# Attention and spectral mixing on one core: one PSUM layout for two parts, and three early score pairs

## The chip, the cores and the metric

The kernel runs on one core of one Trainium2 chip. The metric is the device time of one execution in microseconds; the time before is the median of three runs. A profile of one more execution gives start and duration of every instruction. In its rows PE is the matrix engine TensorE (PEld its weight loads), DVE VectorE, ACT ScalarE, POOL GpSimd, SP SyncE, which issues most DMAs.

## The reference, cut to what matters

```python
g = sigmoid((x * gate_w).sum(-1, keepdims=True))          # x: 1 x 2048 x 512
# A: softmax attention, 32 heads of 16
q, k, v = split_heads(x @ wqkv)
o = softmax(q @ k.T * 16 ** -0.5) @ v
a = merge_heads(o) @ wo
# B: real part of a 2-d Fourier transform, as products with given matrices
p, r = x @ dft_hid_re.T, x @ dft_hid_im.T
b = dft_seq_re @ p - dft_seq_im @ r
out = g * a + (1 - g) * b
```

## The kernel before

All work is written out by hand in one order per engine; each engine runs its own queue in that order, and waits are put in where a tile is read, written or handed on.

**Precision.** Operands of the projections and of the spectral products are split into a high and a low part (`hi`, `lo`), and a product is made of three matmul pairs: hi·hi, hi·lo, lo·hi. `halves_of` (L175) issues such a pair: the two halves of the contraction go to two row groups of TensorE and write two PSUM banks.

**Part one, projections and spectral products** (from L209). Queries, keys and values are projected; the hidden transform is made; then the loop over `coef` (L552) multiplies blocks of the sequence matrices, in units of four key blocks (`u`, `CS = 4`), into a pair of banks `xy`. After a row block's last unit the two banks are scaled by `1 - g` and moved out, the first by ACT (`tx`, L598), the second by ACT or, for the last block, by DVE (`ty`, L600); POOL adds them (`mixed`, L546) and SP stores the sum. Eight row blocks (`LATER`) are left for the attention loop.

**Scans.** Softmax needs an upper bound of each query's scores. A scan is a pair of score matmuls with a DVE maximum behind it (L130, L132; the folded form L149 to L155 shares it between ACT and DVE). There are 64 per pair of heads, 1024 in all; `beside` places the first 692 (`FRONT`) between the products of part one, the attention loop does the other 332.

**Part two, the attention loop** (L884 on): 512 steps, one for each pair of heads `p`, half `h` of the queries and key block `kb`. A step does, in TensorE's order:

- first scores (`c = 0`): a matmul pair into a pair of banks (`s3`), and one exponential over both (ACT, 128 x 1024, `eb`, L649);
- a scan, while there are scans left, into the bank pair `s1`;
- second scores (`c = 1`): a matmul for `j = 0` and one for `j = 1` into two single banks (`s2`, a pool of three), and two exponentials of 128 x 512 (`e`, L653). They run in the order `j = 1`, `j = 0`;
- the value products of the step before (`pv`, L660), four accumulating matmuls with their four column groups in one bank, `pvb`.

From step 333 (`MIX`) there are no scans; every step takes a piece of filling work from `outputs` instead: 128 pieces of three spectral pairs, then pieces of the output projection (`mix_heads`: for the first, third and fifth row block four pieces of 2, 2, 2 and 3 pairs, else two of 4 and 5; then `mix_some`, three pairs each). An even step takes its piece ahead of its scores, an odd step behind them, and the even step does the value products of two steps (`flush` twice, L932).

**PSUM before.** Each part has pools of its own on the eight banks. Part one: `psf`, twice the pair `xy`, and four banks which the projections use as two pairs and the folded scans as four single ones (`psk`: d0, d1, k0, k1). Part two: `ps2`, with the pairs `s1` and `s3`, three banks `s2`, and `pvb`. A pool that is opened waits for those whose place it takes. In the program as built, `s2` gives `j = 0` two banks by turns and `j = 1` one and the same third bank in every step, so a `j = 1` score waits for the `j = 1` exponential of the step before (a later wait is on the `pv` matmul that reads `e` of `j = 0`).

**SBUF before.** Split coefficients lie in eight tiles (`chi`, `clo`, four each) of a pool that ends with part one; the loop has four tiles `eb` and seven tiles `e` of its own.

Of the kernel before, what the change touches and what calls it, by code (L numbers as in the profile page):

```python
# [25 lines left out]
ND = D // P  # L26
NC = S // 512
VC = DH + 1
SCALE = DH ** -0.5
# [6 lines left out]
FRONT = 564 + 16 * LATER  # L36
# [5 lines left out]
MIX = TOTAL - FRONT + 1  # L42
OUT = MIX + NB * LATER
SLOW = 3


def build(tc, x, xT, wqkv, wo, wrT, wiT, cr, ci, gate, out):
    nc = tc.nc
    with ExitStack() as ctx:
        keep = ctx.enter_context(tc.tile_pool(name="keep", bufs=1))  # L50
        stk = ctx.enter_context(tc.tile_pool(name="stk", bufs=6))
        sm = ctx.enter_context(tc.tile_pool(name="sm", bufs=2))
        big = ctx.enter_context(tc.tile_pool(name="big", bufs=1, reuse_waits="tile"))
        dram = ctx.enter_context(tc.tile_pool(name="dram", bufs=1, space=DRAM))

        q_d = [dram.tile([P, 2, S], F32, name=f"q_d{f}") for f in range(ND)]
        k_d = [dram.tile([P, 2, S], F32, name=f"k_d{f}") for f in range(ND)]
# [24 lines left out]
        scanned, used, unfolded = {}, {}, {}  # L82
# [99 lines left out]
        def block(i):  # L182
            return big.tile([P, 512], F32R, tag=f"b{i}", name=f"b{i}")

        ah, al = {}, {}


        seen, slots, due, count = [0], [0], [], [0]
        pace = [None, 0.0]
        with ExitStack() as pf:  # L190
            psf = pf.enter_context(tc.tile_pool(name="psf", bufs=2, space=PSUM))
            cw = pf.enter_context(tc.tile_pool(name="cw", bufs=4, reuse_waits="tile"))

            def s1():
                return pss1[0].tile([P, 2, 512], F32, tag="s1", name="s1")
# [1 line left out]
            pss1 = []  # L197

            def xy():
                ps = psf.tile([P, 2, 512], F32, tag="xy", name="xy")  # L200
                return ps[:, 0, :], ps[:, 1, :]

            def after(n, f, *args):

                count[0] += 1
                due.append((slots[0] + n, count[0], f, args))
# [45 lines left out]
            beds = []  # L252
# [41 lines left out]
            coef = []  # L294
# [4 lines left out]
            coef = coef[:len(coef) - NU * LATER]  # L299
# [7 lines left out]
            def prepare(n, copy=nc.gpsimd.tensor_copy, sub=nc.gpsimd.tensor_sub):  # L307
                if n >= len(coef):
                    return
                hi, lo = (cw.tile([P, 512], F32R, tag=tag, name=tag + "_").rearrange("p (c q) -> p c q", q=P)  # L310
                          for tag in ("chi", "clo"))
                raw = craw.pop(n)
                copy(hi, raw)
                sub(lo, raw, hi.bitcast(F32))
                ready[n] = hi, lo

            with ExitStack() as px:
# [11 lines left out]

                def new_cw():  # L330

                    return [[cw.tile([P, 512], F32R, tag=tag, name=tag + "_") for d in range(ND)]
                            for tag in ("chi", "clo")]

                def split_w(w, d, raw, engine=nc.vector, cols=slice(0, 512)):
                    split(w[0][d][:, cols], w[1][d][:, cols], raw[:, cols], engine)
# [188 lines left out]
                    project_s(wi, t, -1.0, use)  # L525
                run_due(True)

            with ExitStack() as py:
                cp = py.enter_context(tc.tile_pool(name="cp", bufs=2, reuse_waits="tile"))
                def fetch(n):  # L530
                    if n < len(coef):
                        load_coef(n, cp.tile([P, CS, P], F32, tag="craw", name="craw", bufs=5))

                psk = py.enter_context(tc.tile_pool(name="psk", bufs=1, space=PSUM, reuse_waits="tile"))
                beds += [lambda tag: psk.tile([P, 512], F32, tag=tag, name="s"), cp]
                for n in range(4, 8):
                    fetch(n)
                for d in range(4):
# [3 lines left out]
                pss, yre, early = {}, {}, {}  # L542
# [8 lines left out]
                for n, (ph, t, u) in enumerate(coef):  # L551
# [11 lines left out]
                    hi, lo = ready.pop(n)  # L563
# [21 lines left out]
                    for w in range(CS):  # L585
                        s = u * CS + w
                        for i, (c_, a_) in enumerate(((hi, ah[s]), (hi, al[s]), (lo, ah[s]))):
                            halves_of(pss[t], c_[:, w, :], a_, s == 0 and i == 0, s == NB - 1 and i == 2)
                            beside()
                        if swap:  # L590
                            if s == 7:
                                for i in range(8, 11):
                                    early[i] = load_operand(1, i, cp)
                            after(1 + 3 * (s % 8), renew, s)
                    if u == NU - 1:
                        tx = cp.tile([P, D], F32, tag="tx", name="tx")
                        ty = cp.tile([P, D], F32, tag="ty", name="ty")
                        nc.scalar.mul(tx, pss[t][0], gm[:, t:t + 1])  # L598
                        if n == len(coef) - 1:
                            nc.vector.tensor_scalar_mul(ty, pss[t][1], gm[:, t:t + 1])  # L600
# [5 lines left out]
        assert seen[0] == FRONT, seen[0]  # L606

        with ExitStack() as pa:
            ps2 = pa.enter_context(tc.tile_pool(name="ps2", bufs=1, space=PSUM, reuse_waits="tile"))
            pr = pa.enter_context(tc.tile_pool(name="pr", bufs=1, reuse_waits="tile"))  # L610
            cw = pa.enter_context(tc.tile_pool(name="cw2", bufs=2, reuse_waits="tile"))
            ap = pa.enter_context(tc.tile_pool(name="ap", bufs=1, reuse_waits="tile"))

            pvb = ps2.tile([P, 512], F32, tag="pv", name="pvb")
            nc.vector.memset(pvb, 0.0)
            rb = ap.tile([P, 512], F32, name="rb")
            nc.gpsimd.memset(rb, 1.0)


            both = [pr.tile([P, 2, 512], F32, name=f"eb{i}") for i in range(4)]  # L620
            single = [[pr.tile([P, 512], F32, name=f"e{j}_{i}") for i in range(3 + j)] for j in range(2)]
            turn = [0, 0]

            def pair_banks():
                return ps2.tile([P, 2, 512], F32, tag="s1", name="s1")

            def bank():
                return ps2.tile([P, 512], F32, tag="s2", name="s2", bufs=3)

            def bank2():  # L630
                ps = ps2.tile([P, 2, 512], F32, tag="s3", name="s3")
                return ps, (ps[:, 0, :], ps[:, 1, :])

            def qk2(p, h, kb, c):
                n = turn[c]
                turn[c] += 1
                q0 = h * 1024 + c * 512
                qs, ks = used[p]
                if c == 0:
                    ps, pss = bank2()  # L640
                else:
                    pss = [bank() for j in range(2)]
                for j in range(2):
                    b = 64 * j
                    nc.tensor.matmul(pss[j], ks[b:b + 50, kb * P:(kb + 1) * P],  # L645
                                     qs[b:b + 50, q0:q0 + 512], start=True, stop=True)
                if c == 0:
                    e = both[n % len(both)]
                    nc.scalar.activation(e, ps, AF.Exp, scale=SCALE)  # L649
                    return [e[:, j, :] for j in range(2)]  # L650
                e = [ring[n % len(ring)] for ring in single]
                for j in (1, 0):
                    nc.scalar.activation(e[j], pss[j], AF.Exp, scale=SCALE)  # L653
                return e

            quads = [(c, j, 64 * c + 32 * j) for c in range(2) for j in range(2)]

            def pv(p, h, kb, es):
                for c, j, r in quads:
                    nc.tensor.matmul(pvb[r:r + VC, :], va[:, kb, 2 * p + j, :], es[c][j],  # L660
                                     start=kb == 0, stop=kb == NB - 1, tile_position=(0, r))

            def quotients(p, h):
                ob = ap.tile([P, 512], F32, tag="ob", name="ob", bufs=2)
# [193 lines left out]
            groups = {}  # L858

            def part(t, *ks):  # L860

                if t not in groups:
                    if t in (3, 8):
                        ps = pair_banks()
                        groups[t] = ps[:, 0, :], ps[:, 1, :]
                    else:
                        groups[t] = bank2()[1] if t == 9 else (bank(), pvb if t == 11 else bank())
                for k in ks:
                    mix_rest(t, groups[t], k, k == 0 or 7 < t < 11, k == 2)

# [22 lines left out]
            for step in range(NP * PERIODS):  # L893
                p, i = step // PERIODS, step % PERIODS
# [14 lines left out]
                        load_y(c + 2 * (step > OUT))  # L909
                if step >= MIX and step % 2 == 0:  # L910
                    next(fill)
                es = [qk2(p, h, kb, 0)]
                if step == 0:
                    es.append(qk2(p, h, kb, 1))
                if late:
                    late.pop(0)()
                next_scan()
                if step:
                    es.append(qk2(p, h, kb, 1))
                if step >= MIX and step % 2:  # L920
                    next(fill)
# [87 lines left out]
```

## Time and profile before

| | |
|---|---|
| median of three runs | 1755.48 us (1752.98 to 1757.93) |
| the profiled execution, its own time | 1751.4 us |
| its span, first to last instruction | 1749.6 us |
| granted TensorE clock, mean | 0.995 |
| attention loop, first score to last exponential's start | 695.0 to 1731.9 us |
| last scan of the loop | at about 1325 us |
| HBM traffic | 133 MB read, 64 MB written, 112 GB/s over the span |

A row of the timeline gives start, duration, engine, line of the kernel, operation, output and inputs, and how many instructions it merges; a bracket says how long the engine sat idle before it and what ended the wait. In the groups, the two numbers behind the count are busy time in us and mean ns of one, and then the idle time before them.

### The profile page before, as it was taken

The page shows a single profiled execution, that of the slowest core. Times are in us where ns is not written, and L with a number is a line of the kernel's source. Part 1 is how long each engine was busy: PE and PEld are TensorE (multiplying, and loading weights), DVE is VectorE, ACT ScalarE, POOL GpSimd, SP SyncE. Part 2 cuts the span into 40 slices and gives each one's busy share as a digit, 9 for nine tenths or more (in the row PEclk, how much of TensorE's full clock was granted, in tenths as well). Part 3 has the DMA queues.
Part 4 walks back from the last instruction along what each step waited for, and adds up shares of the span by engine and source line. Part 5 has one row for each costly group of instructions (what it writes and reads, how often), then busy time and mean ns, then how long its engine had stood idle before and what let it go on. Part 6 is the DMA issues. An engine that isn't in the chain of part 4 may idle for free.

```text
span 1749.6 us, 35589 instructions
## 1 busy us (share of the span) xinstructions
PE 1719.9 (98%) x13640; PEld 1021.8 (58%) x13640; DVE 1155.1 (66%) x1876; ACT 1451.9 (83%) x2384; POOL 712.7 (41%) x814
## 2 busy tenths in 40 slices
PE   8999999999999999999999999999999999999998
PEld 6887787888888887333333333333334555555554
DVE  6799999999999887666666666666664212222333
ACT  5445346888887887999999999999999888888885
POOL 3678667555556664032322323232232322322222
PEclk9999999999999999999999999999999999999999
DMA  8782666434354445433232423515313254255612
GB/s 296 254 298 79 190 201 206 121 115 117 104 154 140 139 133 120 74 59 63 58 67 56 82 40 64 95 23 99 78 35 73 64 118 90 68 141 137 177 36 100
DMA packets 126810, 199.55 MB, mean 114 GB/s; under 512 B 54016, under 2 KB 56560, under 8 KB 119728
## 3 DMA queue, kind: packets, MB, share of 16 engines
q1 hardware_dynamic: 84368, 161.02, 34.4%
q0 software_dynamic: 38496, 19.47, 5.2%
q10 hardware_dynamic: 3776, 16.78, 3.6%
q8 instruction: 107, 1.75, 0.4%
q14 instruction: 63, 0.52, 0.1%
HBM read 133.04 MB, written 63.71 MB: 112 GB/s over the span
## 4 chain that ended last, share of the span: by engine, by line
PE 89%; DMA 3%; DVE 3%; POOL 2%; issue 2%; ACT 1%; SPq 0%; DVEq 0%; ACTq 0%; POOLq 0%
PE pvb L660 28%; PE xy L180 21%; PE s L645 19%; PE s L180 8%; PE s L149 7%; PE s L130 6%; DVE mx L132 1%; DMA fa<-ks_d 1%; DMA kf_d<-fa 1%; POOL s L215 1%; DMA raws<-wqkv 0%; DMA raws<-xT 0%; POOL el L215 0%; POOL fa L215 0%; DMA abr<-ab_d 0%
## 5 line engine op out<-in xcount | busy, mean ns | idle before, releaser
L132 DVE TENSOR_REDUCE mx<-s 128x2 f32<-128x1024 f32 x524 | 627.2, 1222 | 207.5 <-PE s L130 207.4
L649 ACT ACTIVATE eb<-s 128x1024 f32<-128x1024 f32 x512 | 579.3, 1131 | 55.1 <-PE s L645 55.1
L653 ACT ACTIVATE e<-s 128x512 f32<-128x512 f32 x1024 | 610.3, 708 | 0.4 <-PE s L645 0.4
L660 PE MATMUL pvb<-e,va 128*17 128x512 f32 x2048 | 517.3, 598 | 0.0
L660 PE MATMUL pvb<-eb,va 128*17 128x512 f32 x2048 | 517.1, 598 | 0.0
L645 PE MATMUL s<-qs,ks 50*128 50x512 f32 x2048 | 428.1, 438 | 2.3 <-DVE ty L600 1.6
L645 PEld LDWEIGHTS s<-qs,ks 50*128 50x128 f32 x2048 | 212.6, 185 | 372.4 <-ACT eb L649 282.6
L155 DVE CUSTOM_DVE_ANT_0 fold<-s,fold 128x512 f32<-128x512 f32 x500 | 339.1, 690 | 39.0 <-PE s L149 19.4
L153 ACT ACTIVATE fold<-s 128x512 f32<-128x512 f32 x500 | 296.1, 602 | 70.0 <-PE s L149 43.1
L149 PE MATMUL s<-ks,qs 48*128 48x512 f32 x1000 | 223.3, 404 | 7.6 <-DVE mx L155 6.1
L130 PE MATMUL s<-ks,qs 48*128 48x512 f32 x1048 | 221.6, 396 | 3.7 <-DVE mx L132 2.5
L668 POOL DMA_DIRECT2D lc<-ob x124 | 63.1, 515 | 308.2 <-DVE ob L665 307.9
L660 PEld LDWEIGHTS pvb<-eb,va 128*17 128x17 f32 x2048 | 69.2, 96 | 190.2 <-issue 182.0
L149 PEld LDWEIGHTS s<-ks,qs 48*128 48x128 f32 x1000 | 120.9, 184 | 47.6 <-DVE mx L155 18.2
L675 POOL DMA_DIRECT2D r_d<-lc x31 | 18.1, 585 | 294.9 <-DVE lc L674 286.0
L130 PEld LDWEIGHTS s<-ks,qs 48*128 48x128 f32 x1048 | 108.3, 184 | 14.9 <-DVE mx L132 6.0
L180 PE MATMUL xy<-w,b 64*128 64x512 f32 x768 | 105.2, 392 | 0.2 <-ACT s L379 0.2
L401 ACT ACTIVATE tx<-xy 128x512 f32<-128x512 f32 x48 | 28.7, 599 | 78.6 <-PE xy L180 52.5
L754 DVE SCALAR_TENSOR_TENSOR y<-s,g,y 128x512 f32<-128x512 f32 x50 | 36.6, 748 | 76.6 <-PE s L180 76.0
L677 POOL DMA_DIRECT2D rb<-r_d x124 | 60.6, 496 | 63.0 <-DMA r_d<-lc 63.0
L180 PE MATMUL s<-b,chi 64*128 64x512 f32 x542 | 85.2, 390 | 0.3 <-ACT chi L963 0.3
L180 PEld LDWEIGHTS xy<-w,b 64*128 64x128 f32 x768 | 72.5, 186 | 17.6 <-ACT s L379 1.0
(750 smaller groups left out, 2320.4 us busy)
## 6 DMA issues: line engine op xcount, KB each, us to landing
craw<-ci SPq DMA_DIRECT2D x64, 256.0 KB
craw<-cr SPq DMA_DIRECT2D x60, 256.0 KB
ks<-k_d SPq DMA_DIRECT2D x46, 256.0 KB
qs<-q_d SPq DMA_DIRECT2D x46, 256.0 KB
ab_d<-ab SPq DMA_DIRECT2D x32, 256.0 KB
y_d<-y SPq DMA_DIRECT2D x32, 256.0 KB
o_d<-oh POOLq DMA_DIRECT2D x28, 256.0 KB, 9.8
o_d<-ol POOLq DMA_DIRECT2D x28, 256.0 KB, 11.9
```

Source lines behind the costliest of these rows:

```text
L130: nc.tensor.matmul(ps[:, j, :], qs[b:b + 48, qb * P:(qb + 1) * P], ks[b:b + 48, c * 512:(c + 1) * 512], start=True, stop=True)
L132: nc.vector.tensor_reduce(mx[p][:, :, qb, c], ps, axis=AX.X, op=ALU.max)
L149: nc.tensor.matmul(ps, qs[b:b + 48, qb * P:(qb + 1) * P], ks[b:b + 48, c * 512:(c + 1) * 512], start=True, stop=True)
L153: nc.scalar.activation(fold[j], ps, AF.Relu)
L155: nc.vector.tensor_tensor_reduce(out=fold[j], in0=ps, in1=fold[j], scale=1.0, scalar=-3.0e38, op0=ALU.add, op1=ALU.max, accum_out=mx[p][:, ...
L180: nc.tensor.matmul(ps[j], lhs[r], rhs[r], start=first, stop=last)
L645: nc.tensor.matmul(pss[j], ks[b:b + 50, kb * P:(kb + 1) * P], qs[b:b + 50, q0:q0 + 512], start=True, stop=True)
L649: nc.scalar.activation(e, ps, AF.Exp, scale=SCALE)
L653: nc.scalar.activation(e[j], pss[j], AF.Exp, scale=SCALE)
L660: nc.tensor.matmul(pvb[r:r + VC, :], va[:, kb, 2 * p + j, :], es[c][j], start=kb == 0, stop=kb == NB - 1, tile_position=(0, r))
L668: nc.gpsimd.dma_start(lc[32 * n:32 * n + 32, :], ob[r + DH:r + VC, :].rearrange("p (s e) -> p s e", e=16))
L677: nc.gpsimd.dma_start(rb[r:r + DH, :], r_d[p][h][n:n + 1, :].to_broadcast([DH, 512]))
```

## The change

The layout of PSUM is made once, ahead of both parts: `wide0` and `wide1` (two banks each) for the whole kernel, and, when the projections are done, d0, d1, k0, k1 for the rest. `xy` goes round the two wide tiles by `turns`; the loop's scans and filling use `wide0` (`SCANS_IN`), its first scores `wide1`; the second scores go round d1, k0, d0 by `turn`, two a step, so that the bank of `j = 1` is the one that `j = 0` had a step earlier; `pvb` is k1.

Three score pairs with their exponentials move into the last two units of the spectral loop, behind key blocks 9, 12 and 14 (`AHEAD`): both of step 0, and the first scores of step 1. The second scores of step 0 thereby get one exponential of 128 x 1024 instead of two of 128 x 512. The sums' bank is set to zero there, too. In the loop, step 0 only queues its value products, step 1 begins with them and does its second scores ahead of its scan; the scan of step 0 is dropped there, so that all 332 come one step later, and step 332, so far without scan or filling, has the last.

Coefficients (`c`, high and low part in one tile of `ring4`) and `eb` share four SBUF tiles. The last `ty` lies in a buffer of the tag `raw`.

```diff
+SCANS_IN = 0
+AHEAD = (9, 12, 14)
...
+        ring4 = ctx.enter_context(tc.tile_pool(name="ring4", bufs=4, reuse_waits="tile"))
+        psf = ctx.enter_context(tc.tile_pool(name="psf", bufs=1, space=PSUM, reuse_waits="tile"))
...
+        def wide(i, name):
+            return psf.tile([P, 2, 512], F32, tag=f"wide{i}", name=name)
+        def coefficients():
+            t = ring4.tile([P, 2, 512], F32R, tag="c", name="c")
+            return t[:, 0, :], t[:, 1, :]
...
+        def qk_both(p, h, kb, c=0):
+            ps = wide(1 - SCANS_IN, "s3")
+            qk(p, h, kb, c, [ps[:, j, :] for j in range(2)])
+            if len(both) < 4:
+                both.append(ring4.tile([P, 2, 512], F32, tag="c", name="eb"))
+            e = both[ebs[0] % 4]
+            ebs[0] += 1
+            nc.scalar.activation(e, ps, AF.Exp, scale=SCALE)
+            return [e[:, j, :] for j in range(2)]
...
             def xy():
-                ps = psf.tile([P, 2, 512], F32, tag="xy", name="xy")
+                turns[0] += 1
+                ps = wide(turns[0] % 2, "xy")
                 return ps[:, 0, :], ps[:, 1, :]
...
+            psk = ctx.enter_context(tc.tile_pool(name="psk", bufs=1, space=PSUM, reuse_waits="tile"))
+            def narrow(tag, name):
+                return psk.tile([P, 512], F32, tag=tag, name=name)
+            turn = [0]
+            def bank():
+                turn[0] += 1
+                return narrow(("d0", "d1", "k0")[turn[0] % 3], "s2")
...
+                        if n >= len(coef) - 2 and s in AHEAD:
+                            if not ahead:
+                                sums.append(narrow("k1", "pvb"))
+                                nc.vector.memset(sums[0], 0.0)
+                            ahead.append(qk_both(0, 0, int(s == AHEAD[2]), int(s == AHEAD[1])))
...
-                        ty = cp.tile([P, D], F32, tag="ty", name="ty")
+                        ty = cp.tile([P, D], F32, tag="raw" if last else "ty", name="ty", bufs=3 if last else 2)
...
-            pvb = ps2.tile([P, 512], F32, tag="pv", name="pvb")
-            nc.vector.memset(pvb, 0.0)
+            pvb = sums[0]
...
             def pair_banks():
-                return ps2.tile([P, 2, 512], F32, tag="s1", name="s1")
-            def bank():
-                return ps2.tile([P, 512], F32, tag="s2", name="s2", bufs=3)
+                return wide(SCANS_IN, "s1")
...
-                es = [qk2(p, h, kb, 0)]
                 if step == 0:
+                    pend.append((p, h, kb, ahead[:2]))
+                    continue
+                if step == 1:
+                    flush()
+                es = ahead[2:] if step == 1 else [qk2(p, h, kb, 0)]
+                if step == 1:
                     es.append(qk2(p, h, kb, 1))
                 if late:
                     late.pop(0)()
                 next_scan()
-                if step:
+                if step > 1:
                     es.append(qk2(p, h, kb, 1))
```

More of the change, by code (lines that the diff above doesn't have):

```diff
@@ L183, in block, with qk @@
             return big.tile([P, 512], F32R, tag=f"b{i}", name=f"b{i}")
-        ah, al = {}, {}
+        turns = [0]
+        def wide(i, name):
[3 more added lines that the diff above has]
+            return t[:, 0, :], t[:, 1, :]
+        ah, al = {}, {}
+        quads = [(c, j, 64 * c + 32 * j) for c in range(2) for j in range(2)]
+        both = []
+        def qk(p, h, kb, c, pss):
+            q0 = h * 1024 + c * 512
+            qs, ks = used[p]
+            for j in range(2):
+                b = 64 * j
+                nc.tensor.matmul(pss[j], ks[b:b + 50, kb * P:(kb + 1) * P],
+                                 qs[b:b + 50, q0:q0 + 512], start=True, stop=True)
+        def qk_both(p, h, kb, c=0):
[7 more added lines that the diff above has]
+            return [e[:, j, :] for j in range(2)]
+        ebs, ahead, sums = [0], [], []
         seen, slots, due, count = [0], [0], [], [0]
@@ L190, in build @@
         with ExitStack() as pf:
-            psf = pf.enter_context(tc.tile_pool(name="psf", bufs=2, space=PSUM))
-            cw = pf.enter_context(tc.tile_pool(name="cw", bufs=4, reuse_waits="tile"))
             def s1():
@@ L309, in prepare @@
                     return
-                hi, lo = (cw.tile([P, 512], F32R, tag=tag, name=tag + "_").rearrange("p (c q) -> p c q", q=P)
-                          for tag in ("chi", "clo"))
+                hi, lo = (t.rearrange("p (c q) -> p c q", q=P) for t in coefficients())
                 raw = craw.pop(n)
@@ L330, in new_cw @@
                 def new_cw():
-                    return [[cw.tile([P, 512], F32R, tag=tag, name=tag + "_") for d in range(ND)]
-                            for tag in ("chi", "clo")]
+                    return list(zip(*(coefficients() for d in range(ND))))
                 def split_w(w, d, raw, engine=nc.vector, cols=slice(0, 512)):
@@ L532, in fetch @@
                         load_coef(n, cp.tile([P, CS, P], F32, tag="craw", name="craw", bufs=5))
-                psk = py.enter_context(tc.tile_pool(name="psk", bufs=1, space=PSUM, reuse_waits="tile"))
-                beds += [lambda tag: psk.tile([P, 512], F32, tag=tag, name="s"), cp]
+                beds += [lambda tag: narrow(tag, "s"), cp]
                 for n in range(4, 8):
@@ L594, in build @@
                             after(1 + 3 * (s % 8), renew, s)
+                        if n >= len(coef) - 2 and s in AHEAD:
+                            if not ahead:
+                                assert seen[0] == FRONT, (seen, n, s, pace)
+                                sums.append(narrow("k1", "pvb"))
+                                nc.vector.memset(sums[0], 0.0)
+                            ahead.append(qk_both(0, 0, int(s == AHEAD[2]), int(s == AHEAD[1])))
                     if u == NU - 1:
                         tx = cp.tile([P, D], F32, tag="tx", name="tx")
-                        ty = cp.tile([P, D], F32, tag="ty", name="ty")
+                        last = n == len(coef) - 1
+                        ty = cp.tile([P, D], F32, tag="raw" if last else "ty", name="ty", bufs=3 if last else 2)
                         nc.scalar.mul(tx, pss[t][0], gm[:, t:t + 1])
-                        if n == len(coef) - 1:
+                        if last:
                             nc.vector.tensor_scalar_mul(ty, pss[t][1], gm[:, t:t + 1])
@@ L604, in build @@
                 run_due(True)
-        assert seen[0] == FRONT, seen[0]
+        assert seen[0] == FRONT and turns[0] % 2 == SCANS_IN, (seen, turns)
         with ExitStack() as pa:
-            ps2 = pa.enter_context(tc.tile_pool(name="ps2", bufs=1, space=PSUM, reuse_waits="tile"))
             pr = pa.enter_context(tc.tile_pool(name="pr", bufs=1, reuse_waits="tile"))
@@ L612, in build @@
             ap = pa.enter_context(tc.tile_pool(name="ap", bufs=1, reuse_waits="tile"))
-            pvb = ps2.tile([P, 512], F32, tag="pv", name="pvb")
-            nc.vector.memset(pvb, 0.0)
+            pvb = sums[0]
             rb = ap.tile([P, 512], F32, name="rb")
             nc.gpsimd.memset(rb, 1.0)
-            both = [pr.tile([P, 2, 512], F32, name=f"eb{i}") for i in range(4)]
             single = [[pr.tile([P, 512], F32, name=f"e{j}_{i}") for i in range(3 + j)] for j in range(2)]
-            turn = [0, 0]
+            turn1 = [0]
             def pair_banks():
-                return ps2.tile([P, 2, 512], F32, tag="s1", name="s1")
-            def bank():
-                return ps2.tile([P, 512], F32, tag="s2", name="s2", bufs=3)
-            def bank2():
-                ps = ps2.tile([P, 2, 512], F32, tag="s3", name="s3")
-                return ps, (ps[:, 0, :], ps[:, 1, :])
+                return wide(SCANS_IN, "s1")
             def qk2(p, h, kb, c):
[L635 to L638, printed above, removed]
                 if c == 0:
[L640 to L650, printed above, removed]
+                    return qk_both(p, h, kb)
+                n = turn1[0]
+                turn1[0] += 1
+                pss = [bank() for j in range(2)]
+                qk(p, h, kb, c, pss)
                 e = [ring[n % len(ring)] for ring in single]
@@ L654, in qk2 @@
                 return e
-            quads = [(c, j, 64 * c + 32 * j) for c in range(2) for j in range(2)]
             def pv(p, h, kb, es):
@@ L661, in pv, with bank2 @@
                                      start=kb == 0, stop=kb == NB - 1, tile_position=(0, r))
+            def bank2():
+                ps = wide(1 - SCANS_IN, "s3")
+                return ps[:, 0, :], ps[:, 1, :]
             def quotients(p, h):
@@ L866, in part @@
                     else:
-                        groups[t] = bank2()[1] if t == 9 else (bank(), pvb if t == 11 else bank())
+                        groups[t] = bank2() if t == 9 else (bank(), pvb if t == 11 else bank())
                 for k in ks:
```

## The prediction

> **What bounds the kernel now.** I read the page first: busy time, chain that ended last, costliest groups.
>
> ```profile
> span 1749.6 us, 35589 instructions
> PE 1719.9 (98%) x13640; PEld 1021.8 (58%) x13640; DVE 1155.1 (66%) x1876; ACT 1451.9 (83%) x2384; POOL 712.7 (41%) x814
> PE 89%; DMA 3%; DVE 3%; POOL 2%; issue 2%; ACT 1%; SPq 0%; DVEq 0%; ACTq 0%; POOLq 0%
> L649 ACT ACTIVATE eb<-s 128x1024 f32<-128x1024 f32 x512 | 579.3, 1131 | 55.1 <-PE s L645 55.1
> L653 ACT ACTIVATE e<-s 128x512 f32<-128x512 f32 x1024 | 610.3, 708 | 0.4 <-PE s L645 0.4
> L132 DVE TENSOR_REDUCE mx<-s 128x2 f32<-128x1024 f32 x524 | 627.2, 1222 | 207.5 <-PE s L130 207.4
> ```
>
> TensorE sets the end (98% busy, 89% of the chain), and a pause of TensorE is paid in full unless something else was the limit there. The idle column shows where ACT is nearly a second limit: 0.4 us before all 1024 exponentials of L653. Next, the exponentials of L649 (one per loop step) counted over three stretches: length, busy time (count), granted clock, DMA share, GB/s.
>
> ```profile
> 703.50:1324.50 621.00, 387.54 (x327) 1.00 0.32 62
> 1337.00:1611.50 274.50, 130.30 (x126) 1.00 0.43 101
> 1611.50:1733.00 121.50, 51.45 (x50) 1.00 0.39 104
> ```
>
> Steps with a scan take 621.00 / 327 = 1.899 us; in the next stretch (scans over, spectral products as filling) two steps take 2 x 274.50 / 126 = 4.36. Then the order of time inside a scan step, early and later in the first stretch (start, duration, instruction, count):
>
> ```profile
> 703.92 1.02 ACT L649 ACTIVATE eb<-s 128x1024 f32<-128x1024 f32 x1 [0.63 <-PE s L645]
> 704.85 1.08 ACT L653 ACTIVATE e<-s 128x512 f32<-128x512 f32 x2
> ...
> 800.43 1.24 ACT L649 ACTIVATE eb<-s 128x1024 f32<-128x1024 f32 x1
> 801.35 1.30 ACT L653 ACTIVATE e<-s 128x512 f32<-128x512 f32 x2
> 801.78 0.50 PE L645 MATMUL s<-qs,ks 50*128 50x512 f32 x2
> 802.12 0.39 PE L130 MATMUL s<-ks,qs 48*128 48x512 f32 x2
> 802.33 1.25 ACT L649 ACTIVATE eb<-s 128x1024 f32<-128x1024 f32 x1
> 802.35 0.40 PE L645 MATMUL s<-qs,ks 50*128 50x512 f32 x2
> 802.68 0.61 PE L660 MATMUL pvb<-eb,va 128*17 128x512 f32 x2
> 802.71 0.61 PE L660 MATMUL pvb<-e,va 128*17 128x512 f32 x2
> 803.68 0.50 PE L645 MATMUL s<-qs,ks 50*128 50x512 f32 x2
> ```
>
> TensorE has no gap: first scores 801.78, scan 802.12, second scores 802.35, value products 802.68, next first scores 803.68. ACT is as full: an unhindered pair of exponential groups ends 704.85 + 1.08 = 705.93, 2.01 after its start; at 800 it ends 801.35 + 1.30 = 802.65, 2.22 after, because one queues behind the other. The second scores run at 802.35, 0.30 before that exponential is done.
>
> **The change, part by part.** *The three banks of the second scores.* This part is not in the title and decides the forecast. In every step the second scores (c = 1) take two banks, j = 0 then j = 1, and the exponentials read j = 1 first, j = 0 last. As the kernel before is built, its pool gives j = 0 two banks by turns and j = 1 always the same third one, so the j = 1 score waits for the earlier of the two exponentials of the step before. After the change the banks go strictly round (`turn % 3`, two per step): the j = 1 bank is the one that j = 0 had in the step before, so that score waits for the last exponential. Behind it in TensorE's queue stand the value products and the next first scores, and ACT waits for these. The trace of before shows a j = 1 score really waiting, in a few late steps whose filling is short:
>
> ```profile
> 1611.39 1.08 ACT L653 ACTIVATE e<-s 128x512 f32<-128x512 f32 x2
> 1612.03 0.18 PEld L645 LDWEIGHTS s<-qs,ks 50*128 50x128 f32 x1 [0.19 <-ACT e L653]
> 1612.46 0.10 PEld L660 LDWEIGHTS pvb<-eb,va 128*17 128x17 f32 x2 [0.25 <-issue]
> L653 ACT ACTIVATE e<-s x1024: 588/708/837, 696.7 to 1731.9; 128x512 f32<-128x512 f32 x171
> ```
>
> An exponential alone takes 0.60 (minimum 588 ns), so the first of the two ended at about 1611.99; the weight load of the j = 1 score began at 1612.03 and the value products 0.43 after that. So a score that waits costs 0.04 + 0.43: value products start 0.47 after the exponential it waits for. When nothing waits they start 802.68 - 802.35 = 0.33 after the scores.
>
> Scan steps: the circle is last exponential of step k-2, j = 1 score of k-1, value products, first scores of k, exponentials of k. Its pieces: 0.47; 1.00 from value products to first scores (802.68 to 803.68); 0.55 from first scores to their exponential (801.78 to 802.33); 2.01 to the last exponential (unhindered, since ACT then has gaps). 4.03 per two steps, 2.015 a step against 1.899: 0.116 x 327 = **37.9 us**. If the weights were loaded during the wait (0.33 for 0.43) it would be 1.965 and 21.6; if each wake-up took the 0.11 between 800.43 + 1.24 = 801.67 and 801.78, instead of 0.04, 11 more. I take 37.9, by the row of the same wait. The 2.22 of a full ACT is no upper end: at 2.0 a step ACT, which now does a step in 1.899, cannot stay behind.
>
> Filling steps: value products of two steps follow the second scores of the even step.
>
> ```profile
> 1400.13 0.73 PE L645 MATMUL s<-qs,ks 50*128 50x512 f32 x4
> 1400.67 1.03 ACT L649 ACTIVATE eb<-s 128x1024 f32<-128x1024 f32 x1 [0.47 <-PE s L645]
> 1401.59 1.08 ACT L653 ACTIVATE e<-s 128x512 f32<-128x512 f32 x2
> 1402.08 0.65 PE L645 MATMUL s<-qs,ks 50*128 50x512 f32 x4
> 1402.66 0.61 PE L660 MATMUL pvb<-eb,va 128*17 128x512 f32 x2
> 1404.50 0.73 PE L645 MATMUL s<-qs,ks 50*128 50x512 f32 x4
> ```
>
> The last exponential ends 1401.59 + 1.08 = 1402.67; the value products now start at 1402.66, and would at 1402.67 + 0.47 = 1403.14: 0.48 later, with ACT idle (0.47) and nothing to catch up with. The next odd step does not wait: the even step's exponentials end by 1402.08 + 0.55 + 2.01 = 1404.64, its own second scores come 0.33 after 1404.50. So 0.48 per pair wherever six products or fewer lie between odd and even scores: by the code, 64 pairs of spectral filling (128 yields), six of the first mixing pieces (4 or 5 products; their score already waits as at 1612.03, and moves by one exponential, 0.48), three of `mix_some`. Pairs with nine products between have 3 x 0.23 more (802.35 - 802.12 = 0.23 per product) and do not wait. 73 x 0.48 = **35.0 us**; with 0.33 for 0.43, 27.7; with 0.11 wake-ups, 40.
>
> *The border.* What goes: first the wait at the end of the spectral part, then a slow clock (columns of the windows: busy times and counts of PE, PEld, DVE, ACT, POOL, then clock, DMA).
>
> ```profile
> 693.00 0.39 PE L180 MATMUL xy<-b,clo__10815 64*128 64x512 f32 x1
> 693.48 0.69 ACT L598 ACTIVATE tx<-xy,gm 128x512 f32<-128x512 f32 x1 [4.49 <-PE xy L180]
> 694.20 0.75 DVE L600 TENSOR_SCALAR ty<-xy,gm 128x512 f32<-128x512 f32 x1 [4.31 <-ACT tx L598]
> 695.01 0.90 PE L645 MATMUL s<-qs,ks 50*128 50x512 f32 x4 [1.62 <-DVE ty L600]
> 700.46 0.79 PE L645 MATMUL s<-qs,ks 50*128 50x512 f32 x2
> 703.38 0.50 PE L645 MATMUL s<-qs,ks 50*128 50x512 f32 x2
> 705.26 0.50 PE L645 MATMUL s<-qs,ks 50*128 50x512 f32 x2
> 690.00:694.00 4.00, 3.38 (x29) 2.50 (x26) 0.00 (x0) 0.52 (x1) 0.00 (x0) 1.00 0.00 0
> 694.00:698.00 4.00, 2.29 (x10) 1.49 (x12) 2.46 (x3) 2.39 (x5) 2.89 (x3) 0.75 0.00 0
> 698.00:702.00 4.00, 4.00 (x18) 0.98 (x14) 1.50 (x2) 2.50 (x4) 0.13 (x1) 0.50 0.83 225
> ```
>
> Steps 0 to 2 end at 703.38, 9.99 after the products (693.39). Without loss they are three steps of 1.88 (703.38 to 705.26) less one set of value products (1.00) = 4.64, so at most 5.3 is to be had. After: three score pairs of 0.23 push the end of the products to 694.08; their exponentials, and DVE's memset of the sums, run where DVE (0.00) and ACT (0.52 of 4) are idle. From there: value products of step 0 (1.0), second scores of step 1 (0.33). The scan of step 1 needs the bank pair of the last products: `tx` stands behind the third early exponential: that one's scores start 0.93 before the end of the products (0.23 of their own, three products), it starts 0.55 later and holds ACT 0.93 (703.92 to 704.85), so `tx` starts 0.55 after the end, and with `ty` behind it (0.69, 0.75) the banks are free at about 2.0. The next scan waits for DVE's reduction (0.39 and 1.22 with two wake-ups, 1.7 from scan to scan); then second scores and value products (0.23, 0.33, 1.0): step 3 starts at about 694.08 + 2.0 + 1.7 + 1.6 = 699.4, 4.0 earlier. TensorE pauses twice on the way, some 0.7 and 1.1; where the clock falls as now (2.92 for the step from 700.46, 1.04 over 1.88), two such steps leave 1.9. I take **-3**, ends -5.3 and -1.9. The Trainium skill, TensorE: Matmul & The Clock Gate, section Part 1: The HAM clock gate, lets the clock fall only after an idle window of about 3.4 us; by that the gain would be 4.0. The trace does not agree: 0.75 and 0.50 here after a pause of 1.62.
>
> *The rest at nothing.* Score loads: DMA is at 0.00 from 690; the first early pair, 18 products of 0.23 ahead of the end (689.3), can wait 0.7 for them at most. Scans move by one step: step 332, now without scan and filling, gets one pair (0.23, taken 0.2). No DMA is moved, and the orders of SP and POOL stay; the store of the last `y` and the scan loads behind it come with the border. Coefficient halves in one tile, and the new owners of the same banks, change no order on TensorE before the last two units. The tail keeps its waits.
>
> **The sum**, on the profiled execution's own 1751.4 us: 1751.4 - 3 + 0.2 + 37.9 + 35.0 = 1821.5. The median of the runs (1755.48) is 4.1 above it: **1825**. Lower end: -5.3, 21.6 and 27.7 give 1800; upper end: -1.9, 48.9 and 40 give 1843.
>
> **Rivals.** (1) The wait disappears in idle time and only the border counts: 1751.4 - 3 + 0.2 + 4.1 = 1752.7, or 1750.4 with all 5.3. For it: the second scores, 802.35, lie well ahead of the next first scores, 803.68. Against: it holds only if the j = 1 weights are in place when the last exponential ends, and 1612.03 shows the load starting after the wait. (2) Only filling steps pay, ACT's fullness hides the rest in scan steps: 1751.4 - 3 + 0.2 + 35.0 + 4.1 = 1788. For: ACT's 2.22 against 2.01 is 0.21 of slack. Against: the wait delays the value products by 0.47 - (802.68 - 802.65) = 0.44, twice that slack. (3) The many short pauses bring the clock down: one step in eight at the cold 2.92 would add 63 x 1.04 = 66, 1891. Against: clock 1.00 over 1611.50 to 1733, where such waits stand already. The Trainium skill describes this fall for PSUM banks cycled in every iteration (same page, section A second HAM failure mode: psum-queue depth-cycling); the trace of before shows none.
>
> **How the numbers follow.** Forecast 0.84, rivals 0.06, 0.06, 0.04. Range 1800 to 1842, the bounds above; the rivals lie outside it, and 0.04 of the forecast for what the bounds miss. A measurement here tells 0.3% (5.3 us) from no change. Rival 1 straddles that line: faster 0.03, same 0.03, slower 0.94.
>
> **What would show it.** The weight loads of L645 (its line after) waiting for the L653 exponential in nearly all scan steps; a scan step of about 2.0; filling pairs of 4.84; the 1.62 wait gone and step 3 some 3 to 4 earlier. Wrong: scan steps still at 1.90, or pairs at 4.36.

## The result, and the profile after

The change made the kernel slower: 1818.36 us (median of 5 runs, 1817.42 to 1819.92) against 1757.91 us (median of 5 runs of the kernel before beside them, 1752.98 to 1758.38). The ratio on record is 1.0357, interval 1.0344 to 1.0371 (the quotient of these two medians is 1.0344). The profiled execution of the changed kernel took 1819.31 us, at a mean granted clock of 0.998.

The page of the changed kernel (span, busy times, groups, as before). L209 issues the scores, L220 the wide exponentials `eb`, L686 the narrow ones `e`:

```profile
span 1817.5 us, 35504 instructions
PE 1786.3 (98%) x13640; PEld 1056.6 (58%) x13640; DVE 1156.0 (64%) x1876; ACT 1471.4 (81%) x2383; POOL 710.6 (39%) x814
L220 ACT ACTIVATE eb<-s 128x1024 f32<-128x1024 f32 x513 | 527.3, 1028 | 107.1 <-PE s L209 91.3
L686 ACT ACTIVATE e<-s 128x512 f32<-128x512 f32 x1022 | 556.0, 605 | 1.7 <-PE s L209 1.7
```

The share of TensorE says nothing: 98% before, 98% after, although the same 13640 matmuls take 66 us more. Their ends are modelled, and a matmul held back by its weights counts as busy: four score matmuls take 1.15 at 1500.13, in the filling pair shown below, for 0.65 at 1402.08 before. ACT tells more. The means of both exponentials fell (1131 to 1028 ns, 708 to 605 ns), because they no longer queue behind each other, and the idle time before `eb` rose from 55.1 to 107.1 us. ACT had been nearly full and now waits for scores.

Starts of `eb`, one per loop step, in the stretches that answer to the three shown before (scan steps, spectral filling, the rest):

```profile
700.40:1354.50 654.10, 334.04 (x326) 1.00 0.32 59
1369.20:1673.80 304.60, 129.51 (x125) 1.00 0.38 93
1673.75:1798.20 124.45, 51.46 (x50) 1.00 0.38 97
```

A scan step takes 654.10 / 326 = 2.006 us (1.899 before), a filling pair 2 x 304.60 / 125 = 4.874. Taken between the same steps in both traces (starts of `eb`), the span's 67.9 us (1749.6 to 1817.5) divide so:

| stretch | before | after | difference |
|---|---|---|---|
| up to step 3 | 703.92 | 700.52 | -3.40 |
| steps 3 to 329 | 619.11 | 654.08 | +34.97 |
| 329 to 336 | 13.95 | 14.76 | +0.81 |
| 336 to 461, spectral filling | 273.49 | 304.61 | +31.12 |
| 461 to 511, mixing | 120.04 | 124.43 | +4.39 |
| step 511 to the end | 19.1 | 19.1 | 0.0 |

A scan step, timeline after (start, duration, instruction; the bracket is idle time and what ended it):

```profile
798.77 1.02 ACT L220 ACTIVATE eb<-s 128x1024 f32<-128x1024 f32 x1
799.69 1.08 ACT L686 ACTIVATE e<-s 128x512 f32<-128x512 f32 x2
800.66 1.03 ACT L220 ACTIVATE eb<-s 128x1024 f32<-128x1024 f32 x1
800.83 0.18 PEld L209 LDWEIGHTS s<-qs,ks 50*128 50x128 f32 x1 [0.18 <-ACT e L686]
801.25 0.61 PE L691 MATMUL pvb<-eb,va 128*17 128x512 f32 x2
801.58 1.09 ACT L686 ACTIVATE e<-s 128x512 f32<-128x512 f32 x2
802.23 0.50 PE L209 MATMUL s<-qs,ks 50*128 50x512 f32 x2
802.57 0.33 PEld L209 LDWEIGHTS s<-qs,ks 50*128 50x128 f32 x2
802.77 1.02 ACT L220 ACTIVATE eb<-s 128x1024 f32<-128x1024 f32 x1
802.81 0.41 PE L209 MATMUL s<-qs,ks 50*128 50x512 f32 x2
803.15 0.61 PE L691 MATMUL pvb<-eb,va 128*17 128x512 f32 x2
803.69 1.08 ACT L686 ACTIVATE e<-s 128x512 f32<-128x512 f32 x2
```

The circle can be walked. The last exponential ends at 799.69 + 1.08 = 800.77; the weights of the `j = 1` score load at 800.83; value products at 801.25 (0.48 after that exponential); next first scores at 802.23 (0.98); their exponential at 802.77 (0.54); the last exponential ends at 803.69 + 1.08 = 804.77 (2.00). Round in 4.00 us, two steps. The step from 800.66 takes 2.11 and the one before it 1.89, but both contain the wait: the exponentials of 801.58 end at 802.67, and the next value products start at 803.15, again 0.48 behind. Two circles, one of the odd and one of the even steps, run side by side.

A filling pair, timeline after:

```profile
1498.72 1.02 ACT L220 ACTIVATE eb<-s 128x1024 f32<-128x1024 f32 x1 [0.97 <-PE s L209]
1499.64 1.08 ACT L686 ACTIVATE e<-s 128x512 f32<-128x512 f32 x2
1500.13 1.15 PE L209 MATMUL s<-qs,ks 50*128 50x512 f32 x4
1500.78 0.18 PEld L209 LDWEIGHTS s<-qs,ks 50*128 50x128 f32 x1 [0.45 <-ACT e L686]
1501.21 0.61 PE L691 MATMUL pvb<-eb,va 128*17 128x512 f32 x2
1503.60 1.03 ACT L220 ACTIVATE eb<-s 128x1024 f32<-128x1024 f32 x1 [0.98 <-PE s L209]
```

The exponential ends at 1500.72, the value products start at 1501.21, 0.49 later, and the odd step's `eb` waits 0.97 instead of 0.47.

The border, timeline after, then two windows (PE, PEld, DVE, ACT and POOL busy with counts, clock, DMA share, GB/s):

```profile
692.38 0.86 PE L184 MATMUL xy<-b,c 64*128 64x512 f32 x6
692.64 1.02 ACT L220 ACTIVATE eb<-s 128x1024 f32<-128x1024 f32 x1 [0.65 <-PE s L209]
693.56 0.68 ACT L651 ACTIVATE tx<-xy,gm 128x512 f32<-128x512 f32 x1
694.27 0.75 DVE L653 TENSOR_SCALAR ty<-xy,gm 128x512 f32<-128x512 f32 x1 [4.67 <-ACT tx L651]
695.08 0.50 PE L134 MATMUL s<-ks,qs 48*128 48x512 f32 x2 [0.43 <-DVE ty L653]
696.90 0.52 PE L134 MATMUL s<-ks,qs 48*128 48x512 f32 x2 [1.09 <-DVE mx L136]
699.62 0.79 PE L209 MATMUL s<-qs,ks 50*128 50x512 f32 x2
...
694.00:698.00 4.00, 2.48 (x18) 0.93 (x18) 2.51 (x3) 2.44 (x5) 2.82 (x3) 0.91 0.00 0
698.00:702.00 4.00, 4.00 (x24) 1.00 (x16) 1.83 (x2) 2.48 (x5) 0.18 (x1) 0.67 0.85 229
```

From the end of the products (693.24) to the first scores of step 3 (699.62) it is 6.4, where before it was 9.99. The pauses of TensorE are 0.43 and 1.09, and the clock still falls here, for a shorter time.

### The profile page after: what moved, and what is told of

Same layout as the page of the kernel before. It is cut to its first block, busy times and chain, and to the rows that moved or that the text cites. A ratio compares the mean times of both kernels' runs of the same rounds, so it can differ in the third digit from the quotient of the medians.

```text
span 1817.5 us, 35504 instructions
## 1 busy us (share of the span) xinstructions
PE 1786.3 (98%) x13640; PEld 1056.6 (58%) x13640; DVE 1156.0 (64%) x1876; ACT 1471.4 (81%) x2383; POOL 710.6 (39%) x814
## 4 chain that ended last, share of the span: by engine, by line
PE 87%; DMA 3%; DVE 3%; POOL 2%; issue 2%; ACT 2%; SPq 1%; DVEq 0%; POOLq 0%; ACTq 0%
PE pvb L691 27%; PE s L209 21%; PE xy L184 19%; PE s L184 7%; PE s L153 7%; PE s L134 6%; DVE mx L136 1%; DMA kf_d<-fa 1%; DMA fa<-ks_d 1%; POOL s L252 1%; POOL el L252 0%; ACT eb L220 0%; ACT e L686 0%; DMA q_d<-el 0%; DMA raws<-wqkv 0%
## 5 line engine op out<-in xcount | busy, mean ns | idle before, releaser
L220 ACT ACTIVATE eb<-s 128x1024 f32<-128x1024 f32 x513 | 527.3, 1028 | 107.1 <-PE s L209 91.3
L686 ACT ACTIVATE e<-s 128x512 f32<-128x512 f32 x1022 | 556.0, 605 | 1.7 <-PE s L209 1.7
L209 PEld LDWEIGHTS s<-qs,ks 50*128 50x128 f32 x2048 | 253.7, 184 | 437.1 <-ACT e L686 272.0
L209 PE MATMUL s<-qs,ks 50*128 50x512 f32 x2048 | 498.3, 451 | 2.2 <-ACT e L686 1.5
L184 PE MATMUL xy<-b,c 64*128 64x512 f32 x2640 | 417.7, 392 | 0.5 <-ACT c L318 0.5
L184 PEld LDWEIGHTS xy<-b,c 64*128 64x128 f32 x2640 | 297.5, 187 | 17.1 <-ACT c L318 0.8
L350 POOL TENSOR_TENSOR c<-craw,c 128x512 fp32r<-128x512 f32 x92 | 119.8, 1302 | 7.4
L349 POOL CAST c<-craw 128x512 fp32r<-128x512 f32 x92 | 56.3, 611 | 141.2 <-PE xy L184 137.1
```

The costliest lines, as they stand in the source:

```text
L184: nc.tensor.matmul(ps[j], lhs[r], rhs[r], start=first, stop=last)
```

## The experiments

The theory: the order of the three banks costs all that is lost, since the `j = 1` score waits for the last exponential, and the rest of the change gains a little. The rivals: something else in the new layout costs it, such as other owners of banks or shared SBUF (A), or the strict round as such, whichever exponential is read first (B). Every ratio is against runs of the kernel before on the same chip.

### The third bank given back

```diff
-                return narrow(("d0", "d1", "k0")[turn[0] % 3], "s2")
+                n = turn[0] - 1
+                return narrow("k0" if n % 2 else ("d0", "d1")[n // 2 % 2], "s2")
```

> The kernel after, but j = 1 always gets the same bank (k0) and j = 0 takes d1 and d0 by turns. Theory (the j = 1 score waits for the last exponential of the step before, and everything else of the slowdown follows from that wait): scan steps back at 1.90, filling pairs at 4.37; the span falls from 1817.5 by 67.9 and the 3.4 of the border stay won, 1746 to 1747. Rival A (another part of the layout costs, such as the coefficients and exponentials sharing four tiles, or the places of the banks): the steps stay at 2.01 and the pairs at 4.87, span near 1817.

1749.22 us (median of 7), before 1753.73 (median of 13); ratio 0.9972, interval 0.9958 to 0.9985. The windows of `eb` in scan steps and spectral filling, and the wait of the score weights for the narrow exponential (total, times, longest), first of this kernel, then of the changed one:

```profile
702.95:1322.05 619.10, 390.20 (x326) 1.00 0.34 63
1336.00:1609.50 273.50, 129.30 (x125) 1.00 0.42 102
...
PEld s L209 <- ACT e L687: 78.7, 98, 0.9
```

```profile
PEld s L209 <- ACT e L686: 272.0, 446, 1.7
```

With everything else of the change kept, both stretches are back at the times of before (619.11 and 273.49), and 446 waits become 98. Not all of these are the wait of the theory. The list counts idle time of over 0.15 us before a weight load, and 255 of the 446 and 91 of the 98 are loads for first scores, behind the value products. The loads of the `j = 1` scores make 191 of the 446 and 7 of the 98. Rival A falls: the new owners, the shared tiles and the early scores cost nothing in the loop. The span is 1748.7 for the 1746 to 1747 expected: in this profile the spectral products end at 697.15, 3.9 later than in that of the changed kernel, and step 3 follows 5.32 behind them.

### The strict round alone, put into the kernel before

```diff
-                return ps2.tile([P, 512], F32, tag="s2", name="s2", bufs=3)
+                banks[0] += 1
+                return ps2.tile([P, 512], F32, tag=f"s2{banks[0] % 3}", name="s2")
```

> The kernel before with one thing of the change: its three banks of the second scores go strictly round, two a step. Theory: scan steps 2.01, filling pairs 4.87, and no gain at the border, span 1749.6 + 71 = 1821. Rival A: near 1750, since nothing else of the layout is here.

1824.75 us (median of 4), ratio 1.0402, interval 1.0385 to 1.0420. The windows of its `eb`:

```profile
704.70:1358.60 653.90, 334.29 (x326) 1.00 0.32 58
1373.35:1677.80 304.45, 129.36 (x125) 1.00 0.39 92
```

This one line makes the whole loss. Its scan steps and its filling take as long as those of the changed kernel to 0.3 us (653.90 for 654.10, 304.45 for 304.60).

### The same strict round, the exponentials read in the other order

```diff
-                for j in (1, 0):
+                for j in (0, 1):
                     nc.scalar.activation(e[j], pss[j], AF.Exp, scale=SCALE)
```

> The kernel after, banks strictly round as there, but the two exponentials of the second scores run j = 0 first, j = 1 last. The bank that j = 1 takes over was then read by the earlier of the two. Theory: as with the fixed third bank, steps 1.90, pairs 4.37, span 1746 to 1748. Rival B (going round three banks costs by itself, whichever exponential comes first): steps stay at 2.01, span near 1817.

1748.37 us (median of 6), ratio 0.9966, interval 0.9954 to 0.9979. The windows of its `eb`:

```profile
701.20:1321.10 619.90, 384.88 (x326) 1.00 0.34 63
1335.05:1608.55 273.50, 129.30 (x125) 1.00 0.43 102
```

Rival B falls. The banks go round exactly as in the changed kernel; but now the bank that `j = 1` takes is freed by the first exponential, not the last, and the loss is gone. What costs is the order of handing out against the order of emptying.

### The strict round in the scan steps only

```diff
+                n = turn[0] - 1
+                if seen[0] < TOTAL:
+                    return narrow(("d0", "d1", "k0")[turn[0] % 3], "s2")
+                return narrow("k0" if n % 2 else ("d0", "d1")[n // 2 % 2], "s2")
```

> The kernel after with banks strictly round while there are scans (steps to 331) and the fixed third bank in all later steps. Theory, with the two circles independent: scan steps 2.006, filling pairs 4.37, span 1746.5 + 35 = 1781 to 1783. Rival C (the late start of the scan steps carries on into the filling steps, or the filling steps lose more when the scan steps have lost nothing): off by more than 5 from that sum.

1783.32 us (median of 4), ratio 1.0165, interval 1.0149 to 1.0180. The windows of its `eb`:

```profile
699.70:1353.45 653.75, 334.20 (x326) 1.00 0.32 60
1367.70:1641.25 273.55, 129.28 (x125) 1.00 0.43 101
```

The two circles are independent: the scan steps keep their whole loss (2.005 a step), the filling none, so the two terms may be added. The span, 1780.4, lies 0.6 below the expected range.

### The early scores behind the last product

With the third bank given back, the three early score pairs are issued after the spectral loop instead of between its products.

```diff
-                            ahead.append(qk_both(0, 0, int(s == AHEAD[2]), int(s == AHEAD[1])))
...
+        for kb, c in ((0, 0), (0, 1), (1, 0)):
+            ahead.append(qk_both(0, 0, kb, c))
```

> The kernel with the fixed third bank (e1), but the three early score pairs stand behind the last spectral product instead of between the last ones: the layout alone, without the move that the title names. Theory (the border's 4.0 come from filling the wait behind the last product with scores and value products, for which the exponentials must be there): the first value products then wait for the exponentials (0.55 + 2 x 0.93, a score pair for each bank pair waiting for the exponential before it), step 3 starts some 2 to 3 later than in e1, steps stay 1.90 and 4.37; 1 to 2 faster than the kernel before, 1751 to 1753. Rival D (the layout alone gives the border's gain, the early scores nothing): as e1, 1749.

1754.33 us (median of 12), before 1755.4 (median of 20); ratio 0.9996, interval 0.9985 to 1.0007. No gain, a little less than expected. Its border, timeline and windows:

```profile
697.94 0.50 PE L209 MATMUL s<-qs,ks 50*128 50x512 f32 x2 [1.51 <-ACT eb L220]
699.62 0.79 PE L209 MATMUL s<-qs,ks 50*128 50x512 f32 x2 [1.18 <-ACT eb L220]
707.72 0.80 PE L209 MATMUL s<-qs,ks 50*128 50x512 f32 x2
...
698.00:702.00 4.00, 2.82 (x12) 0.57 (x12) 0.35 (x1) 2.05 (x2) 2.83 (x3) 0.64 0.17 64
702.00:706.00 4.00, 3.10 (x18) 1.45 (x18) 1.66 (x2) 2.00 (x3) 0.00 (x0) 0.50 1.11 213
706.00:710.00 4.00, 4.00 (x22) 1.02 (x19) 1.81 (x2) 2.46 (x4) 0.00 (x0) 0.58 0.96 170
```

The three score pairs share one bank pair, so each waits for the exponential before it (1.51, 1.18), now with no product to run meanwhile. The clock falls for longer, and step 3 starts 11.5 after the products. That is 6.2 later than with the third bank given back (5.32), where 2 to 3 were expected: the expectation took 0.93 from one exponential to the next, but scores and exponential take turns, and the three start at 696.87, 698.55 and 700.52; the slow clock adds to it. Rival D is out. The layout, with the early scores behind the products, gives no gain that the runs show; the gain needs the scores between the products.

### The early scores one key block earlier

With the third bank given back, and in another kernel with the exponentials in the other order: `AHEAD = (9, 11, 13)` for `(9, 12, 14)`, so that `tx` would not stand behind the third early exponential.

> The kernel with the fixed third bank (e1), early scores behind key blocks 9, 11 and 13 instead of 9, 12 and 14, so that the third exponential is over before the last product and the scaling of the last products starts with it. Theory: the scan of step 1 waits for that scaling, so step 3 starts 0.4 to 0.5 earlier, measured from the last product (5.3 now, 4.9 then); the time by 0.03%, too little for the runs. Rival E (the reductions of the scans set the border, not the scaling): still 5.3.

> The kernel with the exponentials in the order j = 0, j = 1 (e3) and early scores behind 9, 11 and 13. Theory: as e6, within the spread of the runs: 1748, 0.3% below the kernel before, steps 1.90 and 4.37.

The first: 1748.61 us (median of 7), ratio 0.9968, interval 0.9950 to 0.9985. The second: 1747.23 us (median of 8), ratio 0.9963, interval 0.9948 to 0.9979. The border of the first, timeline:

```profile
696.44 0.69 ACT L652 ACTIVATE tx<-xy,gm 128x512 f32<-128x512 f32 x1 [0.36 <-PE xy L184]
697.96 0.50 PE L134 MATMUL s<-ks,qs 48*128 48x512 f32 x2 [0.21 <-DVE ty L654]
701.43 0.50 PE L209 MATMUL s<-qs,ks 50*128 50x512 f32 x2
```

`tx` now waits for the product alone and starts 0.11 after the products' end (696.33), where with the third pair a key block later it started 0.32 after; the first wait of TensorE is 0.21 instead of 0.43. From the products to step 3 it is 5.10 and 5.09 in the two kernels, against 5.32 and 5.31 in the same two with the old places: 0.2 earlier, half of what was hoped, and as much as `tx` moved. The timed runs can't tell so little. Both are faster than both kernels of this case; the second has the lowest median of all, 1747.23, 0.37% below before by the ratio, but by the intervals it can't be told from the other three without the loss (0.9972, 0.9966, 0.9968).

## Why the prediction was right

The forecast was 1825 us with a range of 1800 to 1842; 1818.36 was measured, through the mechanism that was named. Step by step:

- **The bank wait exists, and it is the whole loss.** Shown from both sides: given back, the loss goes; alone in the kernel before, it makes all of it. Rival 1 (the wait vanishes in idle time) and rival 2 (only filling steps pay) are out by the scan stretch alone.
- **Scan steps, +37.9, measured +34.97** (and part of the +0.81 behind them). The circle was put at 4.03 and is 4.00 to 4.01; its pieces came out as 0.48, 0.98, 0.54 and 2.00 for 0.47, 1.00, 0.55 and 2.01. As only the difference from 1.899 counts, 0.02 in 4 is 8% of the term. The choices made there held: weights are not loaded during the wait, and the wake-up is short (0.06 and 0.42 before the value products). The +0.2 for step 332 did not come: with the third bank given back, steps 329 to 336 take 13.96, before 13.95.
- **Filling, +35.0, measured 31.12 + 4.39 = 35.5.** A pair grew by 4.874 - 4.376 = 0.498 for the forecast 0.48. (273.50 over 125 steps gives 4.376; the forecast's 4.36 came from a window with one start more than its length covers. The term was made from the wait and did not use it.)
- **The border, -3, measured -3.4.** The worked-out case with a full clock put step 3 at 5.3 after the products; where the clock stays at 1.00, the third bank given back and the other order of exponentials have 5.32 and 5.31. In the changed kernel's profile the clock fell, and it is 6.4. Of the 3.4, 0.84 lies ahead of the products' end (693.24 for the forecast 694.08), which moves by several us from run to run. So it is partly luck that the term came out so close: the slow clock took 1.1, and products that happened to end early gave most of it back.
- **Rival 3, a falling clock in the loop, did not come**: 1.00 in all three stretches, with a wait in nearly every scan step. The mode that the Trainium skill describes (TensorE: Matmul & The Clock Gate, section A second HAM failure mode: psum-queue depth-cycling) does not appear with these pauses.
- **What was to show it** came as said. Counted in the trace, in 326 of 328 scan steps the weights of the `j = 1` score start to load 0.05 us after the end of the last exponential, and the value products follow 0.47 to 0.49 behind that end. In every second step no idle time stands in the trace, because the load of the `j = 0` weights runs up to that moment (802.57, two loads in 0.33). With the third bank given back, no scan step has such a load behind the last exponential; 264 of 329 have it behind the first. In the later steps it is 74 loads, for the 73 that the term counted.
- **The offset of +4.1 did not carry over**, and it is the larger part of the 6.6 that were missed. Forecast without it 1821.5, profiled execution 1819.31, median 1818.36: the changed kernel's profile stands at its median, that of before stood 6.5 below (1751.4 against 1757.91). The clock does not explain this. The profile of before has the slow clock at the border too, and a mean of 0.995; 11 timed runs of that kernel with the same mean took 1752.14 to 1757.47, all longer. The cause stays open. How far executions differ shows in the end of the spectral products, 693.24 to 697.15 in the profiles of the four kernels that are alike up to there (the changed one, the third bank given back, the other order, the round in the scan steps).
- **The early scores save clock as well.** Of 33 timed runs of the kernel before, 3 had a mean granted clock of 0.997 or more, and of 4 of the strict round alone, 1; of 37 runs of the six kernels with scores between the products, 30 had; of 12 with the scores behind the products, none. The mean counts falls elsewhere too, such as one at 573.40 with the third bank given back. In profiles the clock fell at the border with the long pauses in three kernels of three (before; the strict round alone, 0.89, 0.50 and 0.76 in the windows from 694 to 706; scores behind the products), and with the short ones in one of six. Between scores behind and between the products lie 1754.33 - 1748.61 = 5.7 us on one chip, and 11.53 - 5.10 = 6.4 at the border of their profiles. How much of this is clock and how much the waits alone was not separated.

## What to carry to other kernels

A ring of buffers is right only against the order in which they are emptied. When two results per step go round three banks, ask for each request which reader frees it; the one that is emptied last must not be the one asked for soonest. Here swapping two exponentials, or handing out one bank by a fixed rule, is worth the 71 us that steps 3 to 511 had gained, and no busy share of TensorE shows it.

A wait that looks covered (the score ran 0.30 before the exponential ended, and 1.3 before the next first scores) is paid if it closes a circle through the queue behind it: add the circle's pieces and divide by the steps that it spans. Only the difference from the present period counts, so errors of the pieces come out magnified.

Where a pause sometimes slows the clock, one profile does not show what shortening it saves (6.4 from the products to step 3 in the changed kernel, 5.3 in three others with the same border): compare the granted clocks of the timed runs.

## What was not expected of the hardware

Pauses of the same length at the border went both ways. With 0.43 and 1.09 the clock fell in the changed kernel's profile (0.91 and 0.67 in the windows above) and stayed at 1.00 with the third bank given back, whose border has the same instructions in the same order. The traces show where the difference lies. In each of the nine profiles all changes of the granted clock are whole multiples of 3.41 us apart, on a grid whose place differs from execution to execution. Windows cut on this grid, of the changed kernel and then of the third bank given back (its grid counted back from its change of clock at 576.81):

```profile
693.83:697.24 3.41, 1.90 (x14) 0.78 (x10) 1.98 (x2) 2.52 (x4) 2.06 (x2) 1.00 0.00 0
697.24:700.65 3.41, 3.41 (x18) 0.98 (x14) 1.23 (x1) 1.22 (x3) 0.94 (x2) 0.50 0.56 180
```

```profile
696.28:699.69 3.41, 2.98 (x22) 0.99 (x18) 0.91 (x2) 2.69 (x4) 0.67 (x1) 1.00 0.00 0
699.69:703.10 3.41, 2.33 (x20) 0.96 (x18) 2.29 (x2) 2.14 (x5) 2.34 (x3) 1.00 0.17 68
```

In the first both pauses fell into one window, and TensorE was idle for 3.41 - 1.90 = 1.51 of it; in the second they fell into two, 0.43 and 1.08. At the nine borders the clock fell after windows with 1.51 to 2.23 us of idle time and stayed after windows with at most 1.16. Elsewhere in these traces the two overlap (a fall after 1.36, none after 1.59), so this is no sharp limit. No run moved the pauses against the grid on purpose.

The Trainium skill (TensorE: Matmul & The Clock Gate, section Part 1: The HAM clock gate) has the clock fall after an idle window of about 3.4 us; the falls here came with pauses of 1.62, of 1.51 with 1.18, and once of 0.43 with 1.09, all shorter.
